# One order for the whole kernel, made by a list schedule: linear attention and a SiLU feed forward with pre-layernorms

## The chip, the cores and the metric

One core of a Trainium2 chip runs the whole kernel. The metric is the device time of one execution in microseconds, taken as the median of several; the engines are PE (matrix products), DVE, ACT and POOL (element-wise work) and SP (which issues the DMAs here).

## The reference

x is 2048 rows of 640 values in bf16. The first half is attention without a softmax over rows: 32 heads of 20 values, and per head a small matrix `w_phi` (20 x 20) in front of a feature map.

```python
qkv = (layernorm(x) @ wqkv) ...            # 640 -> 3 x 640, heads of 20
pq, pk = q @ w_phi[h], k @ w_phi[h]
phi_q = concat(softmax(pq), softmax(-pq))  # 40 features a head; phi_k alike
kv, z = phi_k^T v, sum of phi_k over rows
o = (phi_q kv) / (phi_q z + 1e-6)
h = x + o @ wo
out = h + silu(layernorm(h) @ w1) @ w2     # 640 -> 1728 -> 640
```

All keys have to be through before any query can be finished, since kv and z are sums over all rows.

## The kernel before

The rows lie in 16 tiles of 128. In a first stage each tile is normalised (mean and variance on DVE, the inverse deviation on POOL by a power, the normalisation on DVE), transposed (tiles 0 to 3 by PE, the others by a DMA transpose that SP issues) and then multiplied with three weights. `w_phi` is folded into the weights beforehand, so that one product gives q @ w_phi: `transposed` and `transposed_pair` turn 128-column blocks of Wk and Wq round on PE, six overlapping blocks of six heads each (`block_start`, `block_own`), ACT or DVE evacuates them, and `fold` multiplies with the block-diagonal `phi`. For Wk this is done before the first key; for Wq the eleven steps stand in `todo` and the key loop takes one or two per turn (`query_fold`).

The key loop (L589 to L628) does in turn t: the keys of tile t (`keys_in`: 10 products into a pair of PSUM banks and two exps on ACT, of the value and its negative), the inverse sums of the tile before (`keys_pairs`: Ln and Exp on ACT, L349, L350), its values (`values_in`), its sums on DVE (`keys_sums`, L340), a piece of Wq's fold, the scaling of the tile before (`keys_scale`, L355), the products of keys and values of tile t-2 (`keys_values`, L362, summed over all tiles in `kv`), from t = 4 on one tile of queries (`more_queries`), then normalisation and transpose of tile t+3, statistics of tile t+4 and one load of a later weight. So the order on every engine is the order of the calls: the kernel runs under `tc.manual_schedule()`, and each engine takes its instructions in the order in which they are written and waits at each for its data.

After the loop `block_diagonal` masks kv into `KVB`, the PSUM pairs are given back, and six single banks (`half`) take their place. Per tile of attention: `query_sums` and `query_ratio` (DVE; three tiles are done in the key loop), `attend_T` (DMA transpose of the query features), `attend_D` (10 products with KVB; the first of each half is 336 columns wide, to write the whole half, the others 84), `attend_E` (division, DVE), `attend_F` (transpose, by PE for tiles 0 and 1, else by DMA), `attend_G` (product with wo and the residual), `ln2_stats`, `ln2_normal` and `ready` (the second normalisation and its transpose). The start of this stage is written out by hand (L673 to L723).

The feed forward is a list of pieces. A unit is one tile for tiles 0 to 3 and then a pair of tiles; `ffn_up` does 2 or 4 blocks of 128 of the 1728 inner columns for a unit (L511, 128 or 256 columns wide, silu on ACT at L515), `ffn_down` half a tile's output (L524, 14 products of 320 columns; then an add on DVE and, with the second half, the store). `take` and `fill` put pieces between the attention steps by estimated times, and what is left runs at the end (L744).

The buffers that the steps name: `pair_ps` two pairs of PSUM banks, `tr_ps` two banks for transposes, `kv_ps` a pair; `VP` four tiles of values with a column of ones, `Ek` four tiles, `Eq` sixteen, `EqT`, `HnT` and `shT` three each. SP's queue carries all loads, all transposes and the stores.

Of the kernel before, what the change touches and what calls it, by code (L numbers as in the profile page):

```python
# [9 lines left out]
ALU = mybir.AluOpType  # L10
# [3 lines left out]
F32 = mybir.dt.float32  # L14


@with_exitstack
def kernel(
# [61 lines left out]
    WARM = 10  # L80
# [29 lines left out]
    def load_later(n):  # L110
        for _ in range(min(n, len(later_loads))):
            nc.sync.dma_start(*later_loads.pop(0))


    QT = range(4, T - 1)
    QR = (8, 10, 12)
    start_ctx = ExitStack()
    start_ctx.enter_context(tc.manual_schedule())
# [11 lines left out]
    KVB = persist.tile([P, NCH, 16 * HV], BF16, name="KVB")  # L130
    mask = persist.tile([P, NCH // 2, 4, HV], F32, name="mask")

    def later_constants():

        nc.gpsimd.memset(w1_sb[:, :, F : FC * P], 0.0)
        nc.gpsimd.memset(w2_sb[64:P, FC - 1, :], 0.0)

        nc.gpsimd.memset(mask[:], 1.0)
        for c in range(NCH // 2):
            off = P * c - HF * first_head(c)  # L140
# [8 lines left out]
        nc.gpsimd.memset(KVB[:, 0:NCH:5, CV:], 0.0)  # L149

    kv_ps = kv_pool.tile([P, 2, 512], F32, name="kv")
    kv_bf = kv_ps[:].bitcast(BF16).rearrange("p b (c e) -> p b c e", e=P)

    def warm(n):

        for _ in range(n):
            nc.tensor.matmul(
                kv_ps[:, 0, :], ident[:], ident[:].unsqueeze(1).to_broadcast([P, 4, P]),
                start=True, stop=True,
            )  # L160
# [3 lines left out]
    NB = 6  # L164
    BW = 6 * DH

    def block_start(r):
        return min(BW * r, D - P)

    def block_own(r):  # L170
        return 6 * r, min(6 * r + 6, H)

    phi = early.tile([P, NB, BW], BF16, name="phi")

    def phi_blocks():
        pp = ps_pair()
        for r in range(NB):
            lo, hi = block_own(r)
            for h in range(lo, hi):
                p0 = DH * h - block_start(r)  # L180
                nc.tensor.matmul(
                    pp[:, r // 4, (r % 4) * BW + (h - lo) * DH : (r % 4) * BW + (h - lo + 1) * DH],
                    SID[:, P - p0 : 2 * P - p0], WPH[:, h, :],
                    start=True, stop=True,
                )
        pf = phi[:].rearrange("p r f -> p (r f)")
        nc.scalar.copy(pf[:, 0 : 4 * BW], pp[:, 0, 0 : 4 * BW])
        n = H * DH - 4 * BW
        nc.vector.tensor_copy(pf[:, 4 * BW : 4 * BW + n], pp[:, 1, 0:n])

    def transposed(W, WT, r, eng=nc.scalar.copy):
        w0 = block_start(r)
        pt = ps_tr()
        for ce in range(C):
            nc.tensor.transpose(pt[:, ce, :], W[:, ce, w0 : w0 + P], ident[:])
        eng(WT[:, r, :], pt[:, 0:C, :].rearrange("p a b -> p (a b)"))  # L196

    def transposed_pair(W, WT, r, eng, pt):
        for i in range(2):
            w0 = block_start(r + i)  # L200
            for ce in range(C):
                nc.tensor.transpose(pt[:, i, ce, :], W[:, ce, w0 : w0 + P], ident[:])
        eng(WT[:, r : r + 2, :].rearrange("p r (a b) -> p r a b", a=C), pt[:, :, 0:C, :])

    def fold(WT, Wf, ce, eng=nc.scalar.copy, ps=None):
        if ps is None:
            ps = ps_pair()
        for r in range(NB):
            lo, hi = block_own(r)
            for g in range(2):  # L210
                a, b = max(lo, 16 * g), min(hi, 16 * g + 16)
                if a < b:
                    nc.tensor.matmul(
                        ps[:, g, (a - 16 * g) * DH : (b - 16 * g) * DH],
                        WT[:, r, ce * P : (ce + 1) * P],
                        phi[:, r, (a - lo) * DH : (b - lo) * DH],
                        start=True,
                        stop=True,
                    )
        eng(Wf[:, ce, :].rearrange("p (g n) -> p g n", g=2), ps[:, :, 0:HD])  # L220
# [3 lines left out]
    WTk = early.tile([P, NB, D], BF16, name="WTk")  # L224
    WTq = early.tile([P, NB, D], BF16, name="WTq")


    def moments(src, mv, k):
        st = keyp.tile([P, 2, 6], F32, name="st")
        for i in range(2):  # L230
            nc.vector.bn_stats(st[:, i, :], src[:, i * HD : (i + 1) * HD])  # L231
        nc.vector.bn_aggr(mv[:, k, :], st[:])  # L232

    def inv_std(mv, shift):
        rs = keyp.tile([P, 2], F32, name="rs", bufs=8)
        nc.gpsimd.tensor_scalar(  # L236
            out=rs[:, 0:1], in0=mv[:, 0, 1:2], scalar1=EPS, scalar2=None, op0=ALU.add
        )
        nc.gpsimd.tensor_tensor(rs[:, 0:1], rs[:, 0:1], nhalf_t[:], op=ALU.pow)  # L239
        if shift:  # L240
            nc.gpsimd.tensor_scalar(
                out=rs[:, 1:2], in0=mv[:, 0, 0:1], scalar1=rs[:, 0:1], scalar2=-1.0,
                op0=ALU.mult, op1=ALU.mult,
            )
        return rs

    def normal(src, mv, rs, shift):
        xn = keyp.tile([P, D], BF16, name="xn", bufs=4)
        if shift:
            nc.scalar.activation(xn[:], src, AF.Identity, bias=rs[:, 1:2], scale=rs[:, 0:1])  # L250
        else:
            nc.vector.tensor_scalar(  # L252
                out=xn[:], in0=src, scalar1=mv[:, 0, 0:1], scalar2=rs[:, 0:1],
                op0=ALU.subtract, op1=ALU.mult,
            )
        return xn

    def transpose_rows(src, dst, eng):
        pt = ps_tr()
        for c in range(C):  # L260
            nc.tensor.transpose(pt[:, c, :], src[:, c * P : (c + 1) * P], ident[:])  # L261
        eng(dst, pt[:, 0:C, :])  # L262
# [3 lines left out]
    mv1, rs1, xn1 = {}, {}, {}  # L266

    XD = 4

    def ln1_stats(t):  # L270
        mv1[t] = keyp.tile([P, 1, 2], F32, name="mv", bufs=8)
        moments(X[:, t, :], mv1[t], 0)
        rs1[t] = inv_std(mv1[t], False)

    def ln1_normal(t):
        xn1[t] = normal(X[:, t, :], mv1.pop(t), rs1.pop(t), False)

# [500 lines left out]
```

## Time and profile before

| what | value |
| --- | --- |
| median of 3 runs | 260.0 us (259.83 to 260.95) |
| the profiled execution | 260.56 us, span 258.8 us |
| PE busy | 243.5 us, 94% of the span |
| DVE busy | 174.7 us, 67% |
| ACT busy | 109.2 us, 42% |
| POOL busy | 31.8 us, 12% |
| mean granted clock of PE | 0.993 |

The span is the time from the first to the last instruction of the profiled execution. Busy time of PE counts from the start of a product to its modelled end, so that a product which waits in the pipeline counts as busy; what PE really needs is read from long rows of equal products. The chain of waits is followed back from the last instruction, at each step to what released it, and names what set the end. A timeline row is one instruction or a few equal ones in a row; starts of neighbouring rows give the rate at which an engine gets on.

### The profile page before, as it was taken

The page shows a single profiled execution, that of the slowest core. Times are in us where ns is not written, and L with a number is a line of the kernel's source. Part 1 is how long each engine was busy: PE and PEld are TensorE (multiplying, and loading weights), DVE is VectorE, ACT ScalarE, POOL GpSimd, SP SyncE. Part 2 cuts the span into 40 slices and gives each one's busy share as a digit, 9 for nine tenths or more (in the row PEclk, how much of TensorE's full clock was granted, in tenths as well). Part 3 has the DMA queues.
Part 4 walks back from the last instruction along what each step waited for, and adds up shares of the span by engine and source line. Part 5 has one row for each costly group of instructions (what it writes and reads, how often), then busy time and mean ns, then how long its engine had stood idle before and what let it go on. Part 6 is the DMA issues. An engine that isn't in the chain of part 4 may idle for free.

```text
span 258.8 us, 5605 instructions
## 1 busy us (share of the span) xinstructions
PE 243.5 (94%) x2318; PEld 188.7 (73%) x2318; DVE 174.7 (67%) x362; ACT 109.2 (42%) x206; POOL 31.8 (12%) x91
## 2 busy tenths in 40 slices
PE   6889979999999799979999999999999999999994
PEld 2767766676776567859789787787787787887873
DVE  1859997599996479859988674985885544532011
ACT  2269976878879549603023031031131130140420
POOL 2246221111100002011001100100110110110000
PEclk9799999999999999999999999999999999999999
DMA  7980867457631000828843850683353510402001
GB/s 222 385 311 3 184 156 147 114 147 177 125 64 37 3 0 3 125 31 125 157 105 74 105 102 3 152 102 72 86 103 76 90 39 29 95 8 51 25 3 51
DMA packets 56723, 25.13 MB, mean 97 GB/s; under 512 B 49082, under 2 KB 55418, under 8 KB 56698
## 3 DMA queue, kind: packets, MB, share of 16 engines
q1 hardware_dynamic: 56048, 24.75, 43.2%
q8 instruction: 18, 0.29, 0.5%
q10 hardware_dynamic: 650, 0.03, 0.2%
q14 instruction: 7, 0.06, 0.1%
HBM read 10.35 MB, written 2.62 MB: 50 GB/s over the span
## 4 chain that ended last, share of the span: by engine, by line
PE 81%; ACT 11%; DMA 5%; DVE 1%; issue 1%; POOL 0%
PE half L511 23%; PE half L524 22%; PE pair L291 17%; PE half L467 9%; ACT Ek L320 4%; DMA OT<-O 3%; PE half L435 3%; PE half L303 3%; PE kv L362 2%; DMA X<-in_A_x_dram 1%; ACT VP L331 1%; ACT WTq L196 1%; ACT Eq L320 1%; ACT Rk L350 1%; PE tr L261 1%; ACT XnT L262 1%
## 5 line engine op out<-in xcount | busy, mean ns | idle before, releaser
L515 ACT ACTIVATE shT<-half 128x512 bf16<-128x512 f32 (+1 forms) x58 | 33.6, 583 | 109.3 <-PE half L511 109.3
L511 PE MATMUL half<-HnT,w_sb 128*128 128x256 bf16 (+1 forms) x700 | 65.1, 251 | 0.0
L524 PE MATMUL half<-w_sb,shT 128*128 128x320 bf16 x448 | 64.3, 299 | 0.0
L511 PEld LDWEIGHTS <-w_sb 128*128 128x128 bf16 x700 | 56.6, 98 | 5.5
L524 PEld LDWEIGHTS <-shT 128*128 128x128 bf16 x448 | 43.4, 98 | 16.2
L291 PEld LDWEIGHTS <-XnT 128*128 128x128 bf16 x430 | 41.1, 98 | 17.6 <-issue 2.8
L529 DVE TENSOR_TENSOR o_t<-half,X 128x320 bf16<-128x320 f32 x32 | 15.6, 487 | 39.4 <-PE half L524 39.4
L236 POOL TENSOR_SCALAR rs<-mv 128x1 f32<-128x1 f32 x32 | 7.2, 225 | 196.0 <-DVE mv L232 196.0
L231 DVE BATCH_NORM_STATS2 st<-X 128x6 f32<-128x320 bf16 x64 | 28.1, 480 | 4.6 <-DMA X<-in_A_x_dram 4.6
L340 DVE TENSOR_REDUCE Sk<-Ek 128x64 f32<-128x1280 bf16 x16 | 23.4, 1464 | 7.8 <-ACT Ek L320 7.8
L467 PE MATMUL half<-wo_sb,OT 128*128 128x320 bf16 x160 | 24.2, 299 | 2.6 <-DMA OT<-O 2.6
L472 DVE TENSOR_TENSOR X<-half,X 128x320 bf16<-128x320 f32 x32 | 15.3, 488 | 14.9 <-PE half L467 14.9
L291 PE MATMUL pair<-Wv,XnT 128*128 128x320 bf16 x160 | 24.8, 302 | 0.4 <-ACT Ek L320 0.2
L291 PE MATMUL pair<-Wfk,XnT 128*128 128x320 bf16 x160 | 24.4, 299 | 0.5 <-ACT VP L331 0.5
L383 DVE TENSOR_REDUCE Sq<-Eq 128x64 f32<-128x1280 bf16 x16 | 23.4, 1462 | 0.0
L320 ACT ACTIVATE Ek<-pair 128x640 bf16<-128x640 f32 x32 | 20.8, 705 | 3.6 <-PE pair L291 3.2
L467 PEld LDWEIGHTS <-OT 128*128 128x128 bf16 x160 | 15.3, 98 | 8.8 <-DMA OT<-O 3.2
L239 POOL TENSOR_TENSOR rs<-rs,nhalf_t 128x1 f32<-128x1 f32 x32 | 18.2, 569 | 2.7
L320 ACT ACTIVATE Eq<-pair 128x640 bf16<-128x640 f32 x22 | 14.3, 701 | 9.1 <-PE pair L291 9.1
L291 PE MATMUL pair<-Wfq,XnT 128*128 128x320 bf16 x110 | 16.7, 299 | 0.0
L252 DVE TENSOR_SCALAR xn<-X,mv,rs 128x640 bf16<-128x640 bf16 x32 | 14.4, 450 | 3.3 <-POOL rs L239 3.1
L447 DVE TENSOR_TENSOR O<-half,Rd 128x320 bf16<-128x320 f32 x32 | 15.7, 491 | 1.1
(71 smaller groups left out, 185.0 us busy)
## 6 DMA issues: line engine op xcount, KB each, us to landing
out_dram<-o_t SPq DMA_DIRECT2D x16, 160.0 KB, 1.8
w_sb<-in_B_w_dram SPq DMA_DIRECT2D x5, 432.0 KB, 3.5
X<-in_A_x_dram SPq DMA_DIRECT2D x3, 640.0 KB, 10.4
w_sb<-in_B_w_dram SPq DMA_DIRECT2D x3, 480.0 KB, 3.7
Wk<-in_A_wqkv_dram SPq DMA_DIRECT2D x1, 800.0 KB, 5.7
Wv<-in_A_wqkv_dram SPq DMA_DIRECT2D x1, 800.0 KB, 7.5
Wq<-in_A_wqkv_dram SPq DMA_DIRECT2D x1, 800.0 KB, 10.4
wo_sb<-in_A_wo_dram SPq DMA_DIRECT2D x1, 800.0 KB, 13.9
```

Source lines behind the costliest of these rows:

```text
L231: nc.vector.bn_stats(st[:, i, :], src[:, i * HD : (i + 1) * HD])
L239: nc.gpsimd.tensor_tensor(rs[:, 0:1], rs[:, 0:1], nhalf_t[:], op=ALU.pow)
L291: nc.tensor.matmul(ps[:, g, 0:HD], XnT[:, c, t * P : (t + 1) * P], W[:, c, g * HD : (g + 1) * HD], start=(c == 0), stop=(c == C - 1),)
L320: nc.scalar.activation(E5[:, g, :, b, :], ps, AF.Exp, scale=sign)
L340: nc.vector.tensor_reduce(s[:], ek[t][:].rearrange("p (q f) -> p q f", f=DH), axis=AX.X, op=ALU.add)
L383: nc.vector.tensor_reduce(s[:], eq[t][:].rearrange("p (q f) -> p q f", f=DH), axis=AX.X, op=ALU.add)
L447: nc.vector.tensor_tensor(o[:, g], q4[:, :, 0:DH], rd[:].unsqueeze(2).to_broadcast([P, 16, DH]), op=ALU.mult)
L467: nc.tensor.matmul(ps[:, 0:HD], OT[:, c, :], wo_sb[:, c, g * HD : (g + 1) * HD], start=(c == 0), stop=(c == C - 1),)
L511: nc.tensor.matmul(p3[:, i, :], w1_sb[:, c, fc * P : fc * P + P], HnT[u][:, c, 0:n], start=(c == 0), stop=(c == C - 1),)
L515: nc.scalar.activation(shT[u][:, f0:f1, 0:n], p3, AF.Silu)
L524: nc.tensor.matmul(ps[:, 0:HD], shT[u][:, fc, k * P : (k + 1) * P], w2_sb[:, fc, g * HD : (g + 1) * HD], start=(fc == 0), stop=(fc == FC - 1),
L529: nc.vector.tensor_tensor(o_t[:, g * HD : (g + 1) * HD], ps[:, 0:HD], X[:, t, g * HD : (g + 1) * HD], op=ALU.add,)
```

## The change

The steps are no longer called in the order in which they run. Each becomes an entry of a `Plan`: a name, an engine, a booked duration, a rank, the steps that it depends on, and a function that writes its instructions. `Plan.run` then simulates the engines while the kernel is being built: on each engine the step that can begin first is next, the lower rank among those that can begin within 0.1 us of each other; and the function of the chosen step is called. The engines' order in the program is that order. On the chip nothing is decided: each engine runs its list and waits by semaphores.

- Ranks: statistics, normalisation, keys and values of tile t about 10 + t, their inverse sums and scaling before these; Wq's folds 40; attention of tile t 1000 + 10t; queries' products 1500 + t; feed forward 2000 + 10 per unit.
- Wk is loaded in two parts, and Wq before the loads of x's tiles 4 to 15 (now two loads). Wk is turned round by row chunks (`Wk[:, ce, ...]`, five blocks of 128 columns without overlap) and folded as soon as its chunk is there; a fold has six products, two of each half overlapping in their columns, and these add up in PSUM (`phi` has zeros where a head does not belong). Wq's chunks are turned round by five DMA transposes.
- From tile 4 on the first normalisation is done on POOL; from tile 2 on the transpose goes by DMA (before: from 4 on). The second normalisation stays on DVE.
- Three PSUM pairs instead of two and two transpose banks; eight single banks later instead of six.
- `attend`: the first two chunks of a half are 126 columns wide over a zero-filled part of KVB, none is 336 wide.
- The feed forward has 16 units of one tile; `HnT` and `shT` have four buffers; attention may run 3.7 tiles ahead of it (`AHEAD`).

```diff
+class Plan:
+    SLACK = 0.1
+    HOP = 0.15
...
+    def run(self):
+        left = dict.fromkeys(self.steps)
+        while left:
+            best = {}
+            for name in left:
+                at = self.ready(name)
+                if at is None:
+                    continue
+                eng, rank = self.steps[name][0], self.steps[name][2]
+                free = self.free.get(eng, 0.0)
+                key = (max(at, free + self.SLACK), rank)
+                if eng not in best or key < best[eng][0]:
+                    best[eng] = (key, max(at, free), name)
...
+            start, eng = min((b[1], e) for e, b in best.items())
...
+            self.free[eng] = start + us
+            self.ends[name] = start + (us if lands is None else lands) + self.HOP
+            emit()
...
+    nc.sync.dma_start(Wk[:, 0:3], wqkv_v[:, 0:3, D : 2 * D])
+    nc.sync.dma_start(Wk[:, 3:C], wqkv_v[:, 3:C, D : 2 * D])
     nc.sync.dma_start(Wv[:], wqkv_v[:, :, 2 * D : 3 * D])
     load_x(2, 4)
+    nc.sync.dma_start(Wq[:], wqkv_v[:, :, 0:D])
     load_x(4, 8)
+    load_x(8, 16)
+    AT_X = [4.6] * 2 + [11.2] * 2 + [13.8] * 4 + [17.2] * 8
+    AT_WK, AT_WV, AT_WQ, AT_WPH = (6.4, 7.2), 9.3, 12.4, 4.6
...
+    for ce in range(C):
+        add(
+            f"wq{ce}", "SP", 1.21, 20 + ce, [],
+            lambda ce=ce: nc.sync.dma_start_transpose(WTq[:, ce], Wq[:, ce, :]), after=AT_WQ, lands=2.7,
+        )
+    def fold(WT, key, ce):
+        ps = ps_of[key, ce] = ps_pair()
+        for g, rs in ((0, (0, 2, 1)), (1, (2, 4, 3))):
+            for r in rs:
+                lo, hi, at = PB[r]
+                a, b = max(lo, HD * g), min(hi, HD * (g + 1))
+                nc.tensor.matmul(
+                    ps[:, g, a - HD * g : b - HD * g],
+                    WT[:, ce, r, :],
+                    phi[:, at + a - lo : at + b - lo],
+                    start=(r == rs[0]),
+                    stop=(r == rs[-1]),
+                )
...
+    for t in range(T):
+        ahead = t - 3.2 if t > 0 else -10
+        add(f"st{t}", "DVE", 1.06, 10 + ahead, [], lambda t=t: moments(t), after=AT_X[t])
+        add(f"rs{t}", "POOL", 0.8, 10 + ahead, [f"st{t}"], lambda t=t: inv_std(t))
+        ring = [f"xt{t - 4}"] if t > 3 else []
+        if t < XP:
+            add(f"xn{t}", "DVE", 0.42, 10 + ahead, [f"rs{t}"] + ring, lambda t=t: normal(t, nc.vector))
+        else:
+            add(f"xn{t}", "POOL", 2.5, 10 + ahead, [f"rs{t}"] + ring, lambda t=t: normal(t, nc.gpsimd))
...
+            add(
+                f"xt{t}", "SP", 1.21, 10 + ahead, [f"xn{t}"],
+                lambda t=t: nc.sync.dma_start_transpose(xt(t), xn_.pop(t)[:]), lands=2.6,
+            )
...
+            if later_loads:
+                load = later_loads.pop(0)
+                add(f"load{t}", "SP", 0.58, 10 + t, [f"xt{t}"], lambda load=load: nc.sync.dma_start(*load))
...
+        add(
+            f"K{t}", "PE", 1.4, 10 + t, [f"x{t}"] + fks,
+            lambda t=t: project(t, Wfk, "K"), ring=("pair", [[f"ex{t}"]]),
+        )
+        add(f"ex{t}", "ACT", 1.2, 10 + t, [f"K{t}"] + ([f"kv{t - NE}"] if t >= NE else []), lambda t=t: key_exps(t))
+        add(f"su{t}", "DVE", 1.42, 10 + t, [f"ex{t}"], lambda t=t: key_sums(t))
+        add(f"rk{t}", "ACT", 0.54, 5, [f"su{t}"], lambda t=t: key_inverse(t))
+        add(f"sc{t}", "DVE", 0.75, 5, [f"rk{t}"], lambda t=t: key_scale(t))
+        add(
+            f"V{t}", "PE", 1.4, 10.5 + t if t else 3.25, [f"x{t}"] + ([] if t else ["wk4e"]),
+            lambda t=t: project(t, Wv, "V"), after=AT_WV, ring=("pair", [[f"ve{t}"]]) if t else None,
+        )
...
+            f"kv{t}", "PE", 0.39, 9, [f"sc{t}", f"ve{t}", "wk4e"] + ([f"kv{t - 1}"] if t else []),
+            lambda t=t: keys_values(t),
...
+            for k, n in ((0, CW), (2, CW), (4, CV), (1, CV), (3, CV)):
+                c = 5 * g + k
+                a = (first_head(c) - 16 * g) * HV
+                nc.tensor.matmul(
+                    qp[:, a : a + n], ET[:, c, :], KVB[:, c, 0:n],
+                    start=(k == 0), stop=(k == 3),
+                )
...
+    UNITS = [(t, t + 1) for t in range(T)]
...
+        add(
+            f"D{t}", "PE", 0.44, r + 1, [f"qt{t}", "bd0", "bd1"] + free, lambda t=t: attend(t),
+            ring=("half", [[f"E{t}0"], [f"E{t}1"]]), when=halves,
+        )
```

Feed forward may begin only when all sixteen tiles of queries are exponentiated, since its buffers take the place of Wfq and of the transposed x (in the kernel before too).

## Rows read from the trace of the kernel before

**Rows 1.** The page: span and busy times (busy us, share of the span, instructions).

```profile
span 258.8 us, 5605 instructions
...
PE 243.5 (94%) x2318; PEld 188.7 (73%) x2318; DVE 174.7 (67%) x362; ACT 109.2 (42%) x206; POOL 31.8 (12%) x91
```

**Rows 2.** Busy time by stretch: start:end, length, then each engine, clock, DMA.

```profile
25.00:30.00 5.00, 5.00 (x53) 3.86 (x51) 4.93 (x10) 4.97 (x10) 1.29 (x4) 1.00 0.63 130
...
110.00:120.00 10.00, 8.22 (x98) 6.84 (x99) 7.28 (x21) 1.16 (x2) 1.66 (x4) 1.00 0.41 75
```

**Rows 3.** The chain of waits in order of time, key stage: start, us, what.

```profile
26.71 1.20 ACT Ek L320 x2
...
28.98 1.19 ACT WTq L196 x2
...
30.17 1.25 ACT Ek L320 x2
...
51.92 0.38 PE kv L362 x10
...
52.31 2.73 PE pair L291 x20
```

**Rows 4.** The chain of waits, turn to attention.

```profile
107.00 4.74 DMA OT<-O
```

**Rows 5.** The chain of waits, feed forward and end.

```profile
127.58 3.91 PE half L511 x70
...
131.49 0.59 PE half L435 x10
...
132.08 1.90 PE half L524 x14
...
153.22 3.28 PE half L511 x30
...
255.39 0.49 DVE o_t L529
```

**Rows 6.** The timeline of all engines, start: start, us, engine, line, operation.

```profile
5.89 0.56 ACT L187 CAST phi<-pair 128x480 bf16<-128x480 f32 x1 [3.19 <-PE pair L181]
...
9.12 0.67 POOL L551 MEMSET VP<- 128x32 bf16 x4
...
9.21 0.76 DVE L252 TENSOR_SCALAR xn<-X,mv,rs 128x640 bf16<-128x640 bf16 x1 [0.82 <-POOL rs L239]
...
16.91 1.57 PE L291 MATMUL pair<-Wfk,XnT 128*128 128x320 bf16 x10 [0.49 <-ACT VP L331]
...
18.43 0.69 POOL L136 MEMSET w_sb<- 64x640 bf16 x1
...
20.73 1.52 PE L291 MATMUL pair<-Wfk,XnT 128*128 128x320 bf16 x10
```

**Rows 7.** The timeline of DVE, key stage.

```profile
23.64 0.81 DVE L355 TENSOR_TENSOR Ek<-Ek,Rk 128x1280 bf16<-128x1280 bf16 x1
...
27.12 0.82 DVE L355 TENSOR_TENSOR Ek<-Ek,Rk 128x1280 bf16<-128x1280 bf16 x1
...
27.85 0.44 DVE L252 TENSOR_SCALAR xn<-X,mv,rs 128x640 bf16<-128x640 bf16 x1
...
28.21 0.88 DVE L231 BATCH_NORM_STATS2 st<-X 128x6 f32<-128x320 bf16 x2
...
29.25 1.43 DVE L340 TENSOR_REDUCE Sk<-Ek 128x64 f32<-128x1280 bf16 x1
...
30.59 0.82 DVE L355 TENSOR_TENSOR Ek<-Ek,Rk 128x1280 bf16<-128x1280 bf16 x1
```

**Rows 8.** The timeline of POOL, key stage.

```profile
23.42 0.57 POOL L239 TENSOR_TENSOR rs<-rs,nhalf_t 128x1 f32<-128x1 f32 x1
```

**Rows 9.** DMA issues: out<-in, engine, operation, count, KB, median us to landing.

```profile
wo_sb<-in_A_wo_dram SPq DMA_DIRECT2D x1, 800.0 KB, 13.9
...
XnT<-xn SPq DMA_TRANSPOSE x12, 2.6
```

More of the change, by code (lines that the diff above doesn't have):

```diff
@@ L170, in block_own @@
-    def block_own(r):
-        return 6 * r, min(6 * r + 6, H)
-    phi = early.tile([P, NB, BW], BF16, name="phi")
-    def phi_blocks():
[L176 to L180, printed above, removed]
+    add("pad1", "POOL", 0.4, R, [], lambda: nc.gpsimd.memset(w1_sb[:, :, F : FC * P], 0.0), after=20.0)
+    add("pad2", "POOL", 0.7, R, [], lambda: nc.gpsimd.memset(w2_sb[64:P, FC - 1, :], 0.0), after=20.0)
@@ new lines @@
+    add("mask", "POOL", 0.5, R, [], lambda: nc.gpsimd.memset(mask[:], 1.0), after=20.0)
+    for c in range(NCH // 2):
+        for side in range(2):
+            add(f"mask{c}{side}", "POOL", 0.3, R, ["mask"], lambda c=c, side=side: mask_of(c, side))
+    add("zeros", "POOL", 0.5, R, [], lambda: nc.gpsimd.memset(KVB[:, :, CV:CW], 0.0), after=20.0)
+    masks = ["zeros"] + [f"mask{c}{side}" for c in range(NCH // 2) for side in range(2)]
+    NB = 5
+    PA = 380
+    PN = 820
+    HEADS = {0: (0, 7), 4: (25, 7), 1: (6, 7), 3: (19, 7), 2: (12, 8)}
@@ new lines @@
+    PB = {0: (0, 240, 0), 4: (400, 640, 140), 1: (120, 260, 380), 3: (380, 520, 520), 2: (240, 400, 660)}
+    phi = early.tile([P, PN], BF16, name="phi")
+    ps_of = {}
+    def phi_blocks():
+        pp = ps_of["phi"] = ps_pair()
+        nc.tensor.matmul(pp[:, 0, 140:240], SID[:, 0:P], WPH[:, 0:5, :], start=True, stop=True)
+        for r, (h0, n) in HEADS.items():
+            for h in range(h0, h0 + n):
+                at = DH * h - PB[r][0] + PB[r][2]
+                b, at = (0, at) if at < PA else (1, at - PA)
+                p0 = DH * h - P * r
@@ L205, in fold @@
[L205 to L220, printed above, removed]
+    add("phi", "PE", 1.2, 1, [], phi_blocks, after=AT_WPH, ring=("pair", [["phi_a", "phi_b"]]))
@@ new lines, with query @@
+    for b in range(2):
+        add(f"bd{b}", "DVE", 0.85, 6 + b, [f"kv{T - 1}"] + masks, lambda b=b: block_diagonal(b))
+    eq, sq, eqt = {}, {}, {}
+    def query(t):
+        if pools["half"] is None:
+            project(t, Wfq, "Q")
+        else:
+            for g in range(2):
+                project_half(t, Wfq, "Q", g)
+    def query_exps(t):
+        eq[t] = pools["att"].tile([P, H * HF], BF16, name="Eq", bufs=T)
+        if ("Q", t) in ps_of:
+            exps(eq[t], ps_of.pop(("Q", t)), 2)
+        else:
+            for g in range(2):
+                exps(eq[t], ps_of.pop(("Q", t, g)), g)
@@ new lines, with use_late @@
+            add(f"h{t}", "ACT", 0.62, 50 + t, [f"ht{t}"] + free, lambda t=t: hn_copy(t))
+        else:
+            add(f"ht{t}", "SP", 1.21, r, [f"hn{t}"] + free, lambda t=t: hn_transpose(t), lands=2.7)
+            add(f"h{t}", "none", 0.0, 0, [f"ht{t}"], lambda: None)
+    outs, shT = {}, {}
+    def use_late(ends):
+        if f"qe{T - 1}" in ends and pools["half"] is not None:
+            proj_ctx.close()
+            pools["late"] = ctx.enter_context(
+                tc.tile_pool(name="late", bufs=1, side="right", reuse_waits="tile")
+            )
+            return True
```

789 lines of the change are left out of this document (370 added, 419 removed).

## The prediction, made before the result was known

> **What bounds the kernel now.** First the page's busy times: PE is busy 243.5 of 258.8 us [rows 1]. That share says little, since it counts waiting matmuls too, so I went on to the stretches: from 25 to 30 us ACT and DVE are both full (4.97 and 4.93 of 5 us), with PE's 5.00 beside them partly waiting time; from 110 to 120 us no engine is full and PE still has holes, 8.22 of 10 us [rows 2]. Then the chain of waits, in order of time. Up to about 43 us it runs over ACT: one lap of the key loop is 3.46 us (26.71 to 30.17), of which two evacuations of Wq transposes take 1.19 [rows 3]. From 43 us the chain is PE with small gaps, and at the turn to attention it leaves PE for a transpose by DMA: 4.74 us, during which PE has only one piece of feed forward [rows 4]. From 125.5 us to the last matmul at 255.4 the chain names PE and nothing else; rows of it give PE's clean rates [rows 5].
>
> With these rates I count the work that PE has left when it starts the keys of tile 2, at 20.73 us [rows 6]. Ten matmuls of 320 columns take 1.36 us (2.73 for 20 [rows 3]). Projections: 14 K, 14 V, 16 Q, 44 x 1.36 = 59.8. Key-value products 16 x 0.38 = 6.1 [rows 3]. Attention 16 x 0.59 = 9.4, out projection (the same form as a projection) 16 x 1.36 = 21.8. Feed forward up: four tiles alone at 3.91, six pairs at 70 x 0.109 = 7.64 (3.28 for 30), together 61.5; down 32 x 1.90 = 60.8 [rows 5]. Wq's 30 transposes at 0.056 (3.91 / 70) 1.7, its five folds about 0.30 each 1.5, five tile transposes of 0.28 1.4. Sum 224.0, so PE would end at 244.7 if it never waited. It ends at 255.4: **10.7 us are lost after 20.73**. Counting the same way inside stretches: 3.7 up to 43 us (ACT), 1.1 up to 75 us, 3.0 at the end of the keys, 2.9 in the ramp up to 125.5. Behind the last matmul stand 3.4 us (258.8 - 255.4: one DVE add and the store).
>
> **The change part by part.**
>
> PE work. Attention drops from 1344 to 1008 columns a tile (its two 336-wide products become 126-wide): 0.59 x 1008 / 1344 = 0.44, saving 16 x 0.15 = 2.3. Feed forward goes to single tiles: 16 x 3.91 = 62.6, so +1.1. Wq's PE transposes go: -1.7. A fold now streams 920 columns instead of 640, by the 1.36 per 3200 columns 0.39 instead of 0.30: +0.5 for Wq. The transpose of tile 3's x goes to DMA: -0.3. Sum 224.0 - 2.7 = **221.3 us** after the start of K2.
>
> Narrow matmuls are the place where a rule speaks against the change. The row shows 70 matmuls of 128 columns, each with its own weight load, in 3.91 us, 55.9 ns each, against 109 ns for 256 columns [rows 5]: two narrow ones cost 2.7 ns more than a wide one, and 420 pairs make the +1.1. The Trainium skill, "TensorE: Matmul & The Clock Gate", section Back-to-back issue gap, gives about 81 ns for sustained matmuls of 128 columns with their weight loads. By that, an estimate, the 840 new narrow matmuls would cost 68 instead of 47 us and the kernel would lose 20 us; the row has the very instructions of this kernel, so I go by the row.
>
> Wait of ACT. The six evacuations of Wq leave ACT, so a key lap there is 3.46 - 1.19 = 2.27 [rows 3], below PE's own lap of K, V and kv, 2.73 + 0.38 = 3.11.
>
> DVE. In the old lap the order is scale 0.73, normalise 0.36, statistics 1.04, sums 1.34, from start to start, 3.47 in all (27.12 to 30.59) [rows 7]. With normalise on POOL from tile 4 on the lap is 3.11: DVE stays as full as PE, without slack of its own. The queries' sums for tiles 0 to 2 remain in it, as before.
>
> POOL. It gets twelve normalisations of 640 columns, which no row shows there. From below: a POOL memset of 640 columns, 0.69 [rows 6]. From above: a read, two operations and a write at that memset's rate, 4 x 0.69 = 2.8, and one DVE scale of 0.82 [rows 7] waited for, 3.6. The plan in the diff books 2.5, nearest to the upper row; I take 2.5. With 0.8 for the inverse deviation (0.57 of it the power [rows 8]) a POOL lap is 3.3. Tile 4's normalisation can begin at about 17 us; twelve laps and a landing of 2.6 [rows 9] put x15 at about 58 us. PE has 4.5 us of work per tile if queries fill, so POOL is covered, and some 12 queries (16 us) are left when the keys end. At 0.69 nothing is gained beyond this, since DVE and PE stand at 3.11; at 3.6 the lap is 4.4, still under 4.5.
>
> Start. Wk by row chunks needs five evacuations and five folds split over ACT and DVE instead of being taken one column block after another, and K0 comes behind V0 alone. ACT has eight copies before K0 (two of phi, x0, two of Wk, three folds), about 0.6 each (1.19 for two [rows 3]), 4.8 us from 5.9 on, where phi's first one began [rows 6]; with a wait or two K0 comes at about 11.5 instead of 16.91 [rows 6]. That is not all gain: before it V0 and V1 were done, now V0 alone. V0, K0, K1, V1 are through at about 15.6. Then K2 waits for x2, which now goes by DMA. Its normalisation is ready at about 14.5, 2.6 more make 17.4. But the transposes are queued on SP behind Wq and the last x loads, and the load of wo, issued last of the first loads, took 13.9 us to land [rows 9]; with Wq's first transposes ahead of it too x2 may land at 20 to 21. I take K2 at **19.5** (bounds 17.4 and 21), 1.2 earlier than before. PE idles some 3 us there, with one or two folds of Wq to cover it.
>
> Stalls after K2, by the four places: ACT's 3.7 go; late next are POOL and DVE, whose laps are covered by queries only where the plan's times hold: 1.5 left. The 1.1 become 0.5 (three PSUM pairs instead of two). End of keys 3.0 becomes 1.0, and ramp 2.9 becomes 1.0: the way from the last key-value product to the first feed forward is about 11 us of DVE, ACT and PE steps, and 12 queries and the next tiles' attention cover it. New, 0.5 at the very end: the last unit is one tile, and its down projection waits for its own last silu. Sum **4.5** (bounds: 0.5, since the stretch after 125 us shows that PE can run without a stall, and the old 10.7).
>
> SP and its queue: seven more transposes (five of Wq, x2 and x3), all early; a load of w1 or w2 follows each x transpose as before, and nothing in the feed-forward stage changes in number.
>
> Sum: 19.5 + 221.3 + 4.5 + 3.4 = 248.7 us of span. The profiled execution took 260.56 for its span of 258.8, so 1.8 lie around it, and it stood 0.56 above the median of 260.0: 248.7 + 1.8 - 0.5 = **250.0 us**.
>
> **The rivals.**
>
> A, *POOL and DVE block each other*. DVE's scale multiplies two tensors in SBUF while POOL reads and writes SBUF 2.5 us of each lap. For it: DVE's normalisation at 9.21 us took 0.76 instead of 0.44, beside POOL memsets that ran from 9.12 to 9.79 [rows 6, 7]. Against it: the scale at 23.64 took its usual 0.81 beside a POOL power from 23.42 to 23.99 [rows 7, 8], though that touches one column. If the scale waits half of POOL's 2.5 us in 0.6 of the laps, twelve laps lose 9 us of DVE; queries cover about half, but the order on PE is written down beforehand and PE stands where it is told to wait: +5, **255**. The Trainium skill, "SBUF — State Buffer", section Who interferes with whom, states this: a DVE instruction with two SBUF inputs and a GpSimd one that reads SBUF exclude each other for a whole instruction; by that rule this rival holds.
>
> B, *POOL becomes the bound* (the slower side). Place: x4 to x15. PE's other work up to K15 lasts from 19.5 to about 82 (26 K and V 35.4, 15 Q 20.4, kv and folds 7). If a normalisation takes 5 us, twice the entry, x15 lands at 17 + 12 x 5.8 + 2.6 = 89: PE idles 6 to 7 us before K15, and has hardly a query left for the way from K15 to the first feed forward, some 15 us, of which it covers 6: 7 more lost than I book. 250 + 6.5 + 7 = **263**. It decides from about 4.8 us; the rows' upper end is 3.6.
>
> C, *everything holds*, x2 lands at 17.4 and the stalls are 2: 250 - 2.1 - 2.5 = **245.5**.
>
> D, *the written order misses the real times*, and PE loses again what it loses now: 10.7 instead of 4.5 and K2 at 21, 250 + 6.2 + 1.5 = 257.7, up to no change where the turn to attention is worse, **259.5**. Durations in the plan near those of the rows (K 1.4 against 1.36, kv 0.39 against 0.38) speak against it; those of DVE and of the early landings are a little short.
>
> **How the numbers follow.** Forecast (248 to 253) 0.50, A 0.20, B 0.11, C 0.09, D 0.10, half of it within 0.5% or beyond. A measurement of this kernel can tell about 0.5% (1.3 us) from no change. Faster 0.50 + 0.20 + 0.09 + 0.05 = 0.84; same 0.04; slower 0.11 + 0.01 = 0.12. The range runs from C to D, 245.5 to 258.0, and leaves out B, the end of D and a little below C.
>
> **What would show it.** Right: the first K matmul near 11.5 us and the third near 19.5; ACT below 80% busy from 25 to 45 us; 1120 narrow up matmuls at 56 ns; POOL normalisations near 2.5 us; no transposing DMA in the chain behind 75 us, and PE without gaps from about 100 us. Wrong: key scales or POOL normalisations whose durations scatter (A); PE waiting for XnT at 40 to 60 us (B); PE waiting for DVE in the key stage while POOL is punctual (D); up matmuls above 60 ns. The prediction fails altogether if the time is above 259.

## The result, and the profile after

The changed kernel takes **253.7 us** (median; 252.26 to 254.95) against 259.7 us for the kernel before in the same runs, a ratio of 0.9742 with the interval 0.9702 to 0.9781: 6.0 us faster. The forecast was 250.0 us, 3.7 us too much gain; the measured time lies inside the stated range of 245.5 to 258.0 and just above the band of 248 to 253 that the forecast itself was given. The profiled execution took 254.95 us, its span 253.2 us.

The page of the changed kernel, with the lines that answer to [rows 1] and the groups that matter (busy us, mean ns of one | idle time before, releaser):

```profile
span 253.2 us, 6387 instructions
...
PE 240.1 (95%) x2689; PEld 192.5 (76%) x2689; DVE 168.3 (66%) x349; ACT 109.0 (43%) x220; POOL 66.2 (26%) x103
...
PE 68%; POOL 17%; DMA 6%; ACT 5%; DVE 2%; issue 1%; POOLq 0%; ACTq 0%
...
L379 POOL TENSOR_SCALAR rs<-mv 128x1 f32<-128x1 f32 x32 | 9.0, 282 | 148.8 <-DVE mv L375 148.7
...
L386 POOL TENSOR_SCALAR xn<-X,mv,rs 128x640 bf16<-128x640 bf16 x12 | 32.6, 2722 | 0.2
```

POOL was busy for 12% of the span before and is now for 26%. In the chain that ended last it had no share before, and has 17% now; this is the line of the kernel before:

```profile
PE 81%; ACT 11%; DMA 5%; DVE 1%; issue 1%; POOL 0%
```

The busy times by stretch show where (columns as in [rows 2]):

```profile
25.00:30.00 5.00, 3.75 (x35) 2.60 (x34) 4.54 (x9) 2.88 (x7) 4.80 (x6) 1.00 1.25 222
30.00:60.00 30.00, 27.47 (x266) 20.20 (x264) 25.24 (x38) 21.69 (x47) 27.85 (x25) 1.00 0.65 177
...
78.00:86.00 8.00, 7.69 (x67) 5.61 (x64) 7.79 (x14) 8.00 (x25) 0.00 (x0) 1.00 0.80 100
...
110.00:120.00 10.00, 10.00 (x120) 8.25 (x117) 9.06 (x21) 2.15 (x5) 0.00 (x0) 1.00 0.86 130
```

From 25 to 30 us ACT has fallen from 4.97 to 2.88 of 5 us and POOL has risen from 1.29 to 4.80: one full engine was exchanged for another. From 110 us PE has no holes any more (10.00 of 10 against 8.22 [rows 2]). The timeline of PE gives the starts that the sum is made of:

```profile
13.84 2.88 PE L435 MATMUL pair<-Wfk,XnT 128*128 128x320 bf16 x20 [0.24 <-DVE Wfk L344]
...
19.84 1.53 PE L435 MATMUL pair<-Wfk,XnT 128*128 128x320 bf16 x10 [0.61 <-DMA XnT<-xn]
...
27.46 1.53 PE L435 MATMUL pair<-Wfk,XnT 128*128 128x320 bf16 x10 [1.25 <-DMA XnT<-xn]
...
66.93 1.53 PE L435 MATMUL pair<-Wfk,XnT 128*128 128x320 bf16 x10 [0.40 <-DMA XnT<-xn]
...
70.04 0.56 PE L335 MATMUL pair<-phi,WTq 128*128 128x240 bf16 x6
70.44 0.71 PE L435 MATMUL pair<-Wfq,XnT 128*128 128x320 bf16 x4
...
86.85 0.62 PE L640 MATMUL half<-KVB,EqT 128*128 128x126 bf16 x10 [1.16 <-ACT OT L666]
...
102.44 1.53 PE L671 MATMUL half<-wo_sb,OT 128*128 128x320 bf16 x10 [0.81 <-DMA OT<-O]
103.81 6.36 PE L781 MATMUL half<-HnT,w_sb 128*128 128x128 bf16 x111
```

K2, the third K, starts at 19.84 (forecast 19.5), the last K at 66.93, the last of Wq's folds only at 70.04 and with it the first query at 70.44: not one query stands between the keys. The chain of waits in order of time (start, us, what) runs over POOL nearly all that while, and gives PE's rates later on:

```profile
17.32 2.52 POOL xn L386
...
31.89 3.66 DMA XnT<-xn
35.55 5.08 POOL xn L386 x2
...
60.57 3.71 POOL xn L386
64.28 0.03 POOL mask L244
64.31 2.58 DMA XnT<-xn
...
66.93 2.89 PE pair L435 x20
...
78.35 5.76 ACT Eq L463 x17
...
90.47 0.45 PE half L640 x10
...
239.98 1.68 PE half L781 x30
...
249.85 0.49 DVE o_t L806
```

The DMA of 3.66 us in it is not what POOL waited for. The normalisation that begins behind it may write its buffer as soon as the transpose of the tile four before it has landed, and that one (issued at 21.72) had: PE used it at 27.46. POOL's own timeline shows what held it there, the statistics of DVE:

```profile
34.19 0.69 POOL L379 TENSOR_SCALAR rs<-mv 128x1 f32<-128x1 f32 x1 [1.48 <-DVE mv L375]
```

PE's work after K2 was forecast at 221.3 us and the tail at 3.4. 253.2 - 19.84 - 221.3 - 3.4 leaves **8.7 us of stalls where 4.5 were booked**. To place them, I took PE's products between two starts at the clean rates (0.136 us for 320 columns, 0.038 for one of kv, 0.45 per 10 of attention, 0.056 for a narrow one, about 0.4 for a fold) off the time between, good to some 0.1 us: 5.1 us are lost from K2 to the last K, 2.9 from there to the first product of feed forward, 0.7 behind it.

### The profile page after: what moved, and what is told of

Its sections match the earlier page's. It is cut to its first block, busy times and chain, and to the rows that moved or that the text cites. A ratio compares the mean times of both kernels' runs of the same rounds, so it can differ in the third digit from the quotient of the medians.

```text
span 253.2 us, 6387 instructions
## 1 busy us (share of the span) xinstructions
PE 240.1 (95%) x2689; PEld 192.5 (76%) x2689; DVE 168.3 (66%) x349; ACT 109.0 (43%) x220; POOL 66.2 (26%) x103
## 4 chain that ended last, share of the span: by engine, by line
PE 68%; POOL 17%; DMA 6%; ACT 5%; DVE 2%; issue 1%; POOLq 0%; ACTq 0%
PE half L781 24%; PE half L797 23%; POOL xn L386 13%; PE half L671 8%; ACT Eq L463 4%; DMA OT<-O 4%; PE pair L435 3%; PE half L640 3%; DMA XnT<-xn 2%; POOL rs L382 2%; PE half L446 2%; PE kv L229 2%; POOL rs L379 1%; PE pair L303 1%; PE pair L335 1%
## 5 line engine op out<-in xcount | busy, mean ns | idle before, releaser
L791 ACT ACTIVATE shT<-half 128x512 bf16<-128x512 f32 (+1 forms) x64 | 34.7, 544 | 107.9 <-PE half L781 107.9
L781 PE MATMUL half<-HnT,w_sb 128*128 128x128 bf16 x1120 | 66.0, 219 | 0.0
L781 PEld LDWEIGHTS <-w_sb 128*128 128x128 bf16 x1120 | 63.9, 98 | 1.1
L435 PEld LDWEIGHTS <-XnT 128*128 128x128 bf16 x360 | 33.7, 98 | 19.2 <-DMA XnT<-xn 6.6
L379 POOL TENSOR_SCALAR rs<-mv 128x1 f32<-128x1 f32 x32 | 9.0, 282 | 148.8 <-DVE mv L375 148.7
L386 POOL TENSOR_SCALAR xn<-X,mv,rs 128x640 bf16<-128x640 bf16 x12 | 32.6, 2722 | 0.2
L435 PE MATMUL pair<-Wv,XnT 128*128 128x320 bf16 x150 | 22.8, 299 | 0.0
L650 DVE RECIPROCAL Rd<-half 128x16 f32<-128x16 f32 x32 | 7.9, 247 | 17.7 <-PE half L640 17.6
L463 ACT ACTIVATE Eq<-half 128x320 bf16<-128x320 f32 x48 | 16.7, 469 | 4.4 <-PE half L446 3.4
L446 PE MATMUL half<-Wfq,XnT 128*128 128x320 bf16 x120 | 17.4, 299 | 0.0
```

Source lines behind the costliest of these rows:

```text
L386: eng.tensor_scalar(out=xn_[t][:], in0=X[:, t, :], scalar1=mv_.pop(t)[:, 0:1], scalar2=rs_.pop(t)[:], op0=ALU.subtract, op1=ALU.mult,)
L435: nc.tensor.matmul(ps[:, g, 0:HD], XnT[:, c, t * P : (t + 1) * P], W[:, c, g * HD : (g + 1) * HD], start=(c == 0), stop=(c == C - 1),)
L446: nc.tensor.matmul(ps[:, 0:HD], XnT[:, c, t * P : (t + 1) * P], W[:, c, g * HD : (g + 1) * HD], start=(c == 0), stop=(c == C - 1),)
L463: nc.scalar.activation(E5[:, g, :, b, :], p4, AF.Exp, scale=sign)
L781: nc.tensor.matmul(p3[:, i, :], w1_sb[:, c, fc * P : fc * P + P], HnT[u][:, c, 0:n], start=(c == 0), stop=(c == C - 1),)
L791: nc.scalar.activation(shT[u][:, f0:f1, 0:n], p3, AF.Silu)
```

## The experiments

Theory: POOL's normalisation sets the pace of the keys, because nothing in PE's written order fills the time. Rivals: the order alone (Wq's folds ranked 40, behind the keys), or the early DMA queue. "Lost" is counted as just above, so a small negative loss is none. Each ratio is against the kernel before.

| kernel | us, ratio (interval) | K2 | last K | queries before it | lost: K2 to last K, to feed forward, behind |
| --- | --- | --- | --- | --- | --- |
| after | 253.7, 0.974 (0.970 to 0.978) | 19.84 | 66.93 | 0 | 5.1, 2.9, 0.7 |
| e1 fills first | 255.0, 0.979 (0.976 to 0.983) | 20.40 | 65.11 | 0 | 3.2, 4.1, 0.8 |
| e2 xn on DVE | 249.1, 0.956 (0.952 to 0.959) | 20.29 | 69.63 | 4 | 1.9, -0.1, 1.0 |
| e3 xn booked longer | 258.6, 0.992 (0.988 to 0.995) | 19.65 | 75.58 | 4 | 8.5, 3.4, 0.8 |
| e4 folds early | 255.7, 0.982 (0.978 to 0.986) | 22.65 | 72.73 | 4 | 2.7, 3.7, 0.6 |
| e5 loads later | 252.9, 0.970 (0.966 to 0.975) | 20.24 | 65.48 | 0 | 3.3, 1.2, 0.8 |
| e6 all booked as measured | 251.3, 0.966 (0.962 to 0.970) | 20.11 | 66.04 | 1 | 2.6, 1.1, 0.8 |
| e7 xn split | 249.4, 0.958 (0.954 to 0.962) | 19.98 | 65.29 | 1 | 2.0, 0.5, 0.3 |
| e8 xn on DVE, x2, x3 by PE | 248.9, 0.955 (0.952 to 0.959) | 19.12 | 68.56 | 4 | 1.2, 1.7, 0.0 |
| e9 xn on DVE, loads later, landings | 247.9, 0.954 (0.951 to 0.957) | 19.93 | 63.59 | 1 | 0.3, 0.5, 0.1 |
| e10 xn split, landings | 249.5, 0.958 (0.955 to 0.961) | 19.88 | 62.90 | 0 | 0.7, 1.0, 0.2 |

**e2: normalisation back on DVE.** `XP` is the first tile that POOL normalises.

```diff
-    XP = 4
+    XP = T
```

> All first normalisations back on DVE, the rest of the plan as it is (it orders anew for the booked 0.42 us). Theory P: the lap becomes DVE's 3.47 us instead of POOL's 3.9, K15 at 62 to 65 although the plan puts three or four queries and all folds of Wq ahead of it, PE loses under 3 us instead of 5.2 in the key stage, and the kernel is 1 to 4 us faster than after. Rival D (the lap is DVE's already): DVE gets 12 x 0.36 = 4.3 us more, K15 beyond 70, 1 to 3 us slower.

249.1 us; by the two ratios 1.85% of 260 us, 4.8 us, below the changed kernel; POOL has left the chain. The chain on its page, then a stretch of this kernel:

```profile
PE 82%; DMA 9%; DVE 5%; issue 1%; ACT 1%; POOL 0%; POOLq 0%
```

```profile
30.00:60.00 30.00, 29.14 (x282) 21.77 (x281) 28.24 (x47) 24.59 (x48) 9.29 (x16) 1.00 0.76 184
```

PE goes from 27.47 to 29.14 of 30 us in the key stage, although DVE now carries the twelve normalisations too. So this part of the change costs time. But the plan, which sees other durations, also put four queries before the last K; pace and order changed together.

**e1: pace alone.** POOL's fills and masks may run first, not between the normalisations.

```diff
-... memset(w1_sb[:, :, F : FC * P], 0.0), after=20.0)
+... memset(w1_sb[:, :, F : FC * P], 0.0), after=2.0)
-... memset(w2_sb[64:P, FC - 1, :], 0.0), after=20.0)
+... memset(w2_sb[64:P, FC - 1, :], 0.0), after=2.0)
-... memset(mask[:], 1.0), after=20.0)
+... memset(mask[:], 1.0), after=2.0)
-... memset(KVB[:, :, CV:CW], 0.0), after=20.0)
+... memset(KVB[:, :, CV:CW], 0.0), after=2.0)
```

> The fifteen small POOL fills (two pads, the mask's memset and ten selects, the zeros of KVB) may run from 2 us on instead of from 20, so that those which the plan finds room for lie ahead of the twelve normalisations on POOL; no work is added or removed. Theory P (POOL's chain from 17.3 to 64.3 us sets the pace of the keys): some 2 us of fills (0.36 + 0.63 + 0.45 + 0.3 + 0.3) leave that chain, K15 begins 1.5 to 2 us sooner than 66.9 and the kernel is 1 to 2 us faster. Rival D (DVE's lap of statistics, sums and scale sets the pace, and POOL only follows it): K15 stays within 0.5 us of 66.9, no change.

The last K comes 1.8 us sooner, as the theory of pace has it, but the kernel is no faster, where 1 to 2 us were expected. All sixteen queries still stand behind the keys, and the timeline of PE shows a wait at the change from pairs to single banks:

```profile
65.11 1.52 PE L435 MATMUL pair<-Wfk,XnT 128*128 128x320 bf16 x10
...
74.92 8.31 PE L446 MATMUL half<-Wfq,XnT 128*128 128x320 bf16 x60 [1.39 <-ACT Eq L463]
```

ACT evacuates a query in 1.36 us there (24 pieces in 8.18 us in the changed kernel), just PE's own time, so whatever ACT still owes when the row of queries begins is handed on.

**e3: order alone, by booking POOL's steps longer** (2.9 and 0.95 instead of 2.5 and 0.8), and **e4: the same with Wq's folds ranked 11 instead of 40** (the last pair of lines, and alike for their evacuations).

```diff
-add(f"xn{t}", "POOL", 2.5, 10 + ahead, ...
+add(f"xn{t}", "POOL", 2.9, 10 + ahead, ...
-add(f"rs{t}", "POOL", 0.8, 10 + ahead, ...
+add(f"rs{t}", "POOL", 0.95, 10 + ahead, ...
-... f"fq{ce}", "PE", 0.45, 40 + ce / 10, ...
+... f"fq{ce}", "PE", 0.45, 11 + ce / 10, ...
```

> The same work; only the plan's booked times for POOL change, 2.9 instead of 2.5 us for a normalisation and 0.95 instead of 0.8 for an inverse deviation, near the 2.72 and 0.85 of the trace. The plan then sees gaps on PE and puts all five folds of Wq before K7 and four queries between K8 and K15. Theory P with the missing cover (PE stands in the key stage because the written order has nothing else for it): PE loses 2 to 3 us there instead of 5.2, K15 stays near 67 to 70 but four queries are done by then, 2 to 4 us faster. Rival R (the way from the last key to the first feed forward sets the end, whatever PE does before): no change within 1 us, and PE loses the more between the last key and the first feed forward.

> As the run with the booked POOL times, and Wq's folds ranked 11 instead of 40, so that all five stand before V3. Theory P with the missing cover: as that run or up to 1 us better, since the first gaps (1.25 us before K5 and 1.2 before K8 in after) can take work as well: 2 to 5 us faster than after. Rival S (the folds wait for Wq's transposes, which land 5.4 us after their issue at this time, and PE stands there): K2 to K4 come 1 to 2 us later and the gain is below that of the other run.

Both have four queries before the last K, and both are slower than the changed kernel, by the ratios 4.5 us and 2.1 us (the interval of e4 just touches that of the changed kernel). Longer bookings moved a transpose of Wq ahead of x4's on SP, and PE waited 3.68 us for x4. The timeline of e3 and its stretch, then the timeline of e4:

```profile
29.70 2.85 PE L435 MATMUL pair<-Wfk,XnT 128*128 128x320 bf16 x10 [3.68 <-DMA XnT<-xn]
...
34.16 1.52 PE L435 MATMUL pair<-Wfk,XnT 128*128 128x320 bf16 x10
```

```profile
30.00:40.00 10.00, 10.00 (x93) 7.30 (x92) 5.57 (x8) 6.28 (x13) 6.66 (x5) 0.88 1.03 268
```

```profile
18.92 1.72 PE L335 MATMUL pair<-phi,WTq 128*128 128x240 bf16 x12 [3.47 <-DMA WTq<-Wq]
...
22.65 1.52 PE L435 MATMUL pair<-Wfk,XnT 128*128 128x320 bf16 x10
```

In e4 the folds were put where Wq was booked to be there, and PE, which takes its steps in the written order, stood 3.47 us before them and came to K2 2.8 us later than in the changed kernel. My expectation for e3 was wrong: the plan's early landings (2.6 and 2.7 us) were short as well, and a truer entry beside false ones made the order worse. More queries between the keys don't by themselves shorten the turn behind them either (3.4 and 3.7 us lost).

**e5: the early queue alone.** A weight load follows the transpose four tiles later.

```diff
-add(f"load{t}", "SP", 0.58, 10 + t, [f"xt{t}"], ...
+add(f"load{t}", "SP", 0.58, 10 + t, [f"xt{min(t + 4, T - 1)}"], ...
```

> After, with each load of wo, w1 and w2 tied to the transpose of x four tiles later (the first now behind tile 6's instead of tile 2's), so that no large load stands before x4 and x5 in SP's DMA queue. Theory Q (in the early key stage the x transposes wait in the queue behind wo and w1, x4 landed 5.7 us after its issue): K4 comes 1 to 2 us before 27.46; the kernel gains 0 to 1.5 us, less if POOL's chain takes it back. Rival P alone (POOL's normalisations set the pace whatever the queue does): K4 sooner, K8 and K15 unmoved within 0.5 us, no change in the time.

The timelines of SP in the changed kernel, then in e5. Ahead of x4's transpose (at 21.72) there were two loads; in e5 they are gone, and x4's K starts at 26.44 instead of 27.46:

```profile
20.48 0.57 SPq L427 DMA_DIRECT2D wo_sb<-in_A_wo_dram  x1
21.10 0.52 SPq L427 DMA_DIRECT2D w_sb<-in_B_w_dram  x1
21.72 1.47 SPq L422 DMA_TRANSPOSE XnT<-xn  x1
```

```profile
19.55 2.59 SPq L326 DMA_TRANSPOSE WTq<-Wq  x2
22.24 1.22 SPq L422 DMA_TRANSPOSE XnT<-xn  x1
```

The median is 0.8 us lower, but the intervals of the two ratios overlap (0.9702 to 0.9781, 0.9663 to 0.9745).

**e6: POOL still normalises, everything booked as measured** (POOL 2.65 and 0.9, Wq's transposes 5.6, those of x 4.0 and 5.7 for the first six tiles, folds ranked 11).

> After, POOL still normalises; the plan is told what the trace of after shows: 2.65 us for a normalisation, 0.9 for an inverse deviation, 5.6 to landing for Wq's transposes, 4.0 for x2 and x3, 5.7 for x4 and x5, and Wq's folds ranked 11. Theory B (wrong bookings alone made the key stage's holes): 249 to 251 us, as with DVE's normalisation. Rival N (a normalisation on POOL costs by itself: it stands in the way from statistics to keys with 2.5 instead of 0.4 us and follows DVE's every delay): above 252.

251.3, by the ratios 2.1 us below the changed kernel (the two intervals just touch): not quite half of what POOL's normalisation cost comes back by truer bookings and the order that they make, with POOL still normalising. POOL is still 14% of the chain.

**e7: the work divided.** Even tiles from 4 on go to DVE, odd ones to POOL.

```diff
-        if t < XP:
+        if t < XP or t % 2 == 0:
```

> From tile 4 on the first normalisation alternates: even tiles on DVE, odd on POOL. POOL's lap is then half of 3.9 us per tile and DVE's 3.11 + 0.18 on average. Theory N: only POOL's saturation costs, so this is as fast as all on DVE or up to 1 us faster, 248 to 249.5 us. Rival L (each POOL normalisation costs by itself, by its own latency of 2.5 us and by DVE's scale standing before it): between the two, 250.5 to 252.5.

249.4, the time of e2, with only one query before the last K where e2 has four: with half of the load POOL gets through, and hardly any cover is needed.

**e8: e2 with the transposes of x2 and x3 by PE again** (`XD = 4`).

> The normalisations all on DVE, and tiles 2 and 3 of x transposed by PE again as in the kernel before the change, instead of by DMA. In the run with DVE's normalisation K2 came at 20.3 us with PE idle for 2 us before it. Theory Q: without the queue K2 comes at 17.5 to 18.5; PE gets 0.6 us more work (two transposes) and ACT 1.4: 1 to 2 us faster than that run, 247 to 248. Rival A (ACT, which copies both tiles out of PSUM, delays the first keys' exps, and DVE's lap is what counts from there): within 0.7 us of it.

248.9, no change that can be told from e2: K2 starts 1.2 us sooner and the turn behind the keys takes it back (1.7 lost there, against -0.1).

**e9 and e10: the two good placements with true landings**, e9 with e5's later loads too.

```diff
-... after=AT_WQ, lands=2.7,
+... after=AT_WQ, lands=5.6,
-... lands=2.6,
+... lands=4.0 if t < 4 else 5.7 if t < 6 else 2.6,
```

> Normalisation of all tiles on DVE, the loads of weights issued four tiles of x later, and the landings of early transposes booked as measured (5.6 us for Wq; 4.0 and 5.7 for the first six tiles of x). If what is left after moving normalisation back (2.8 us lost behind K2) comes from the early queue, tile 4's wait falls by the 1.0 us that the later loads alone gave and the time goes from 249.1 to about 248.0. If it comes from the turn at the end of the keys (half-bank evacuations of queries on ACT, 0.47 us each), nothing changes: 249 to 249.5. The third K between 19.5 and 20.5 in both.

> Normalisation of even tiles from 4 on by DVE, of odd ones by POOL, with the early landings booked as measured. The split alone gave 249.4. Theory early queue: 248.5, with tile 4 no sooner but more folds of Wq and queries ahead of it. Theory end of keys: 249.5 as before. If the truer bookings move queries ahead of late keys that then come late, 250.5.

e9 is the fastest version, 247.9 us, by the ratios 5.3 us below the changed kernel. Its page and its stretch of 20 to 60 us:

```profile
PE 85%; DMA 10%; DVE 1%; SPq 1%; ACT 1%; issue 1%
```

```profile
20.00:60.00 40.00, 39.83 (x391) 30.18 (x392) 39.57 (x66) 31.73 (x65) 16.14 (x32) 1.00 0.77 166
```

PE is busy 39.83 of 40 us and only 0.9 us are lost behind K2. Its interval overlaps that of e2, so the difference between these two is not shown. e10 is e7 again, within the interval.

**e11: the one part alone, in the kernel before.** Tiles 4 to 15 are normalised by POOL, nothing else (`normal` is given the engine).

```diff
-        xn1[t] = normal(X[:, t, :], mv1.pop(t), rs1.pop(t), False)
+        xn1[t] = normal(..., nc.gpsimd if t >= 4 else nc.vector)
```

> The kernel before, with only this changed: tiles 4 to 15 are normalised by POOL. Theory POOL lap: POOL needs 2.5 to 2.7 us for a normalisation and 0.6 to 0.9 for the power, 3.4 to 3.9 with the hop between engines; the lap of ACT there is 3.46, so the key loop goes to 3.5 to 3.9 a lap and the kernel gets slower by 0 to 5 us, 260 to 265, with POOL in the chain of waits between 25 and 70 us. Rival: ACT's lap of 3.46 hides it and DVE's falls to 3.11, so the time stays within 0.5 us of 260.

260.3 us, ratio 1.0012 (0.9983 to 1.0042): the step costs nothing there that can be told, as the rival had it; in the profiled executions its last K stands at 80.59 us against 79.87. Its group on POOL, then PE's timeline:

```profile
L252 POOL TENSOR_SCALAR xn<-X,mv,rs 128x640 bf16<-128x640 bf16 x12 | 31.0, 2583 | 1.3
```

```profile
44.98 1.52 PE L291 MATMUL pair<-Wfk,XnT 128*128 128x320 bf16 x10
...
49.62 1.52 PE L291 MATMUL pair<-Wfk,XnT 128*128 128x320 bf16 x10
```

From 43.6 us on the hand-written loop puts a query into every turn, so a turn of PE lasts 4.64 us and POOL's normalisation and power, about 3.4, pass beneath it. Before that its turns hold Wq's transposes and folds, and last 4.2 to 6.0 us from one K to the next (3.7 to 6.0 in the kernel before). Such work in every turn is the cover that I had counted on in the changed kernel, and that its written order does not have.

## Why the prediction was wrong in size

The direction and the parts held; one term was mis-sized. By the steps:

- **The step that failed**: "PE has 4.5 us of work per tile if queries fill, so POOL is covered, and some 12 queries (16 us) are left when the keys end", with 1.5 us booked for the stage, and 0.5 for its second part. Measured are 5.1 lost, and all sixteen queries left. Without a query a tile is only 3.1 us of PE's work, less than even the booked lap of 3.3, so POOL decides from there and not from the 4.8 us per normalisation that rival B named. I had read the ranks (keys 10 + t, folds 40) in the diff and not drawn what they mean: a fold ranked 40 goes in only where PE has nothing else that can begin, and the last one came at 70.04.
- **POOL's lap**: booked 3.3, measured (64.28 - 17.32) / 12 = 3.9. A normalisation takes 2.52 undisturbed, as booked, but 2.72 in the mean, 2.4 us more for the twelve, and the small steps of 0.23 + 0.57 some 1.4 more in all, both beside DVE's scales (below); fills and masks add 1.9, and the wait for DVE's statistics shown above 1.5. That is nearly all of the 7.4 us beyond twelve laps of 3.3. Without what the scales cost, an estimate from these numbers, the lap would be 3.6, still above 3.1. x15 landed at 66.9 instead of 58 (the booked numbers, 17 + 12 x 3.3 + 2.6, make 59).
- **Rival A**, the blocking of POOL and DVE, is real, but it is POOL that pays for it, while DVE's key scales up to the last normalisation keep to 0.77 to 0.88 us. As I priced it, through DVE, it did not happen. Its time of 255 lies nearer to the measured one than the forecast does, and that is luck.
- **Rival D** shares in it: the order was made with landings of 2.6 and 2.7 us for early transposes, most of which took 4 to 6.3. x4's wait of 1.25 us is that. e5 takes this wait away, though its time can't be told from the changed kernel's, and e6 gives 2.1 us back.
- **The first K** came at 13.84, not 11.5: the chain up to there is PE itself (transposes, folds and V0, without a hole from 5.0 to 12.9 us) where I had counted ACT's copies only. It cost nothing, since K2 waited for x2 as forecast.
- **The start**, 19.84 against 19.5; **PE's work**, with attention at 0.45 against 0.44 and the narrow products at 1.68 / 30 = 56 ns; **the tail**, 3.4: right. e9 bounds the work: from its K2 to its last product 222.2 us pass, so 221.3 can't be far off. The Trainium skill, "TensorE: Matmul & The Clock Gate", section Back-to-back issue gap, would have the narrow ones at 81 ns; 1120 of them at 56 decide for the row.
- **The turn and the ramp**: 2.9 us lost against 2.0 booked, with two waits of 1.16 (for the copy of tile 0's output, queued on ACT behind evacuations of queries) and 0.81; behind it 0.7 against 0.5.

With normalisation on DVE (e2) the kernel stands at 249.1 us. That is near the forecast of 250.0, but not made up as forecast: K2 is 0.8 us later, and 2.8 us are lost behind it where 4.5 were booked. What stays open is how the 4.8 us divide between POOL's pace and the order that it led to: e7 shows that half of POOL's load off it is enough, e6 that a truer order gives back not quite half, and no run changes one with the other held fixed to the last step. How much of POOL's pace is the blocking by DVE's scales, no run separates either. Nor do the runs say what sets the loss at the turn: it is 3.4 with four queries ahead (e3) and 1.0 with none (e10).

## What to carry to other kernels

A slower engine is covered only by work that stands in the written order at that place; before booking it as hidden, find in the ranks what is really between two of its steps, and compare its lap with the lap of the bound engine without that work. When a list schedule is fed from measurements, correct all entries of a stage together, the early DMA landings first: truer entries for POOL beside false landings cost 4.5 us by the ratios (e3). And test a suspected part in the old kernel as well: the same step cost nothing where it had cover.

## What the hardware showed

**POOL waits for a two-input DVE step, and holds it up only shortly after its own beginning.** POOL's and then DVE's timeline of the changed kernel:

```profile
25.59 2.52 POOL L386 TENSOR_SCALAR xn<-X,mv,rs 128x640 bf16<-128x640 bf16 x1
...
40.61 0.85 POOL L379 TENSOR_SCALAR rs<-mv 128x1 f32<-128x1 f32 x1
...
42.09 0.23 POOL L379 TENSOR_SCALAR rs<-mv 128x1 f32<-128x1 f32 x1
...
60.55 3.73 POOL L386 TENSOR_SCALAR xn<-X,mv,rs 128x640 bf16<-128x640 bf16 x1
```

```profile
26.40 0.77 DVE L491 TENSOR_TENSOR Ek<-Ek,Rk 128x1280 bf16<-128x1280 bf16 x1
...
40.59 0.78 DVE L491 TENSOR_TENSOR Ek<-Ek,Rk 128x1280 bf16<-128x1280 bf16 x1
```

A step of POOL that needs 0.23 us takes 0.85 when DVE's scale has just begun, and ends just behind it. A normalisation that began beside two scales (60.55) took 3.73 instead of 2.52; one that began beside DVE's statistics, which have one input (25.59, the statistics from 25.36 to 26.24), took its 2.52. The other way round, the scale that begins 0.81 us into a normalisation (26.40) takes its usual 0.77. In e11 three scales began 0.31 to 0.52 us after the start of a normalisation; they took 1.03 to 1.24 and each ended 1.55 us after that start. POOL's and DVE's timelines there:

```profile
42.76 2.52 POOL L252 TENSOR_SCALAR xn<-X,mv,rs 128x640 bf16<-128x640 bf16 x1
```

```profile
43.26 1.05 DVE L355 TENSOR_TENSOR Ek<-Ek,Rk 128x1280 bf16<-128x1280 bf16 x1
```

So a normalisation of 2.5 us holds a scale of 0.81 up until 0.74 us (1.55 - 0.81) after its start, and no longer. A scale that comes quickly enough goes first: in e5 one began 0.17 us after a normalisation and took 0.77, and the normalisation took 3.18. POOL's and DVE's timelines of e5:

```profile
29.75 3.18 POOL L386 TENSOR_SCALAR xn<-X,mv,rs 128x640 bf16<-128x640 bf16 x1
```

```profile
29.92 0.77 DVE L491 TENSOR_TENSOR Ek<-Ek,Rk 128x1280 bf16<-128x1280 bf16 x1
```

The Trainium skill, "SBUF — State Buffer", section Who interferes with whom, names just this pair of instructions as one that contends, calls the shared ports an exclusive lock, and says, of DVE's two-port modes, that whoever issues first has them for the whole instruction. If that is taken over to this pair, the runs agree for DVE's scale, which POOL waits out, and not for POOL's normalisation, which lets a scale through after 0.74 of its 2.52 us.

**PE's clock fell after a wait.** In e3 PE stood 3.68 us before x4's K, the granted clock of 30 to 40 us is 0.88 in the mean, and the ten products behind the wait took 2.85 us instead of 1.52: the lower of its two levels (1.2 of 2.4 GHz) for that while. In e4 it fell too: behind the wait of 3.47 us twelve products of a fold took 1.72 us, where twelve take 0.96 in the changed kernel (40.24). The waits of the changed kernel, up to 1.25 us in that stage, left it at 1.00.
